# A second token pair's first feature tiles in seven products of halves instead of plain matmuls

## The chip, the cores and the metric

The kernel runs on one core of a Trainium2 chip, as one program. The metric is the device time of one execution in microseconds, lower is better; of the kernel before there are three runs. A profiled execution of its own gives the trace. Engine names in the rows: PE is TensorE's matmuls and PEld its weight loads, DVE is VectorE, ACT is ScalarE, POOL is GpSimd, SP is SyncE, whose queue issues every transfer here.

## The reference

```python
# attention: q, k, v are (4, 8, 576, 64) fp32
scores = (q @ k^T) / sqrt(64)
ret = (scores * Dmat) @ v               # Dmat[h, i, j] = gamma_h ** (i - j) where i >= j, else 0
x = ret, all heads side by side         # 2304 tokens x 512
# first layer, w_in 512 x 2048, w_out 2048 x 512
h = x @ w_in
x = (h * sigmoid(h)) @ w_out
# second layer, same sizes
h = x @ w_in2
g = max(h, 0) + alpha * min(h, 0)       # alpha: one number per feature
out = g @ w_out2
```

All of it is in fp32.

## The kernel before

**Matmuls.** An fp32 operand is kept as two tiles, a high and a low part (`split`: ScalarE casts the high part, VectorE subtracts it to get the low one). A product is three matmuls: high by high, low by high, high by low. The moving operand has 384 columns, half of a *token pair* of 768 tokens; there are three pairs (0, 1, 2).

**Feature tiles.** The 2048 features are 16 tiles of 128, taken two at a time (q = 0 to 7); two q make a group, and each layer has four groups. For one q and one token pair, 512 x 256 weights against 512 x 768 tokens, the work is done in one of two ways. *Plain* (`h_unit`): twelve matmuls for each of two feature tiles and two token halves, 48 in all. *Seven products of halves* (`products`): the weights and the tokens are cut in halves both ways, sums of the quarters are multiplied, seven products of six matmuls each, 42 in all. The weights' sums are made by `sums`, the tokens' seven operands B11, T1, B21, T2, B22, T3, T4 by `operands` (seven `split`s of 768 elements, by `put`, and four differences, by `less`, in place). They live in one set of tiles, `xop`, for the pair that is at work, and are stored to memory (`od`) and loaded again when the pair comes up next. The products share PSUM banks: the first and third use bank a, the second and fifth d, the first (by a copy on ScalarE), fourth, sixth and seventh b. Each must wait until what stood in its bank has been read: the seventh for the addition on VectorE that takes the sixth's result.

**The woven part.** Attention is done in 18 blocks of 128 tokens. Behind each block ScalarE copies the result to `ybuf`. While attention runs, the first group (four feature tiles) of pairs 0 and 1 is computed by plain units between the blocks, and then the output units y, twelve matmuls each that multiply activations by `w_out`. For this, `keep` (L548) splits each block of pairs 0 and 1 into its plain operands and stores it to memory (`xd`), from which `operands_again` makes the seven operands when the pair comes up in the second group. Pair 2 never has plain units: its operands are made by `operands` in the late part. The order on TensorE is written out in `EARLY_ORDER` and `LATE_ORDER` (L38 to L40) and followed by `follow`: `b` is a whole attention block (its first outputs, the next block's loads, scaling and scores, the next block's state, its second outputs), `h10` is one plain unit of pair 1's first half, `y01` one output unit of pair 0's second half, `s` the weights' sums for q = 0 and 1, `o` the operands of pair 2. `close_att` stands between the two orders: it gives back the attention's memory, in which the following tiles are then laid, among them the buffer `rawb` for weights.

**What sets the order elsewhere.** Every instruction is first recorded. TensorE's stand in the recorded order. For the other engines and SP's queue, `Program.order` plays the program through with rough costs and takes, among what can start, what is due first; each engine then works through its list strictly in that order. Alpha's load and the step that turns it into `nalpha_sb`, which only the second layer reads, are recorded behind the late order, and the planner puts them where they fit.

Of the kernel before, what the change touches and what calls it, by code (L numbers as in the profile page):

```python
# [9 lines left out]
F32 = mybir.dt.float32  # L10
# [8 lines left out]
P = 128  # L19
# [5 lines left out]
NC = DM // P  # L25
# [6 lines left out]
HALF = 384  # L32
NT6 = NT // HALF
NPR = NT6 // 2
BPP = 2 * HALF // P
PACKS = 3
EARLY = 8
EARLY_ORDER = ("w10 f g w4 i w3 l k j i w3 l w1 k j w2 i l j k h00 b h00 b h00 b h00 h01 b "  # L38
               "h01 b h01 b h01 b y00 y00 b y00 b y01 b y00 y01 y01 y01 b h10 h10 b h10 b h10 b b")
LATE_ORDER = "h11 h11 h11 h11 s o y10 y10 y10 y10"  # L40
PERIOD = 2 * S // P
WIDE = 3
SMALL = [C, 2 * C, C, NPAIR * C, P]
# [190 lines left out]
def retention_ffn_kernel(ctx: ExitStack, tc: tile.TileContext, qkv, w1, w2, alpha, small, out):  # L234
# [3 lines left out]
    dram = ctx.enter_context(tc.tile_pool(name="dram", bufs=1, space=bass.MemoryType.DRAM))  # L238
# [3 lines left out]
    nalpha_sb = const.tile([P, NF], F32, name="nalpha_sb")  # L242
    seven = const.tile([P, 1], F32, name="seven")
    ybuf = big.tile([P, NC * NT], F32, name="ybuf")
    xd = [dram.tile([P, NC * 2 * HALF], F32, name=f"xd{p}") for p in range(NPR - 1)]
    od = [[[dram.tile([P, 4 * HALF], F32, name=f"od{l}_{p}_{i}") for i in range(7)] for p in range(NPR)]
          for l in range(2)]

    def f32(t):
        return t.bitcast(F32)  # L250

    def feat(p):
        return ybuf[:, p * NC * 2 * HALF:(p + 1) * NC * 2 * HALF].rearrange("p (c t) -> p c t", c=NC)
# [23 lines left out]
    stock, lent = Store(), {}  # L277
# [18 lines left out]
    banks = [ps.tile([P, 512], F32, name=f"bank{i}") for i in range(4)]  # L296
    homes = {"a": banks[0:1], "b": banks[1:2], "d": banks[2:3], "o": banks[3:4]}
# [45 lines left out]
    def split(hi, lo, src):  # L343
        nc.scalar.copy(hi, src)
        nc.vector.tensor_tensor(out=lo, in0=src, in1=f32(hi), op=ALU.subtract)
# [45 lines left out]
    def sums(both, w):  # L391
        a21, a22, a11, a12 = (w[:, i * 256:(i + 1) * 256] for i in range(4))
        nc.vector.tensor_tensor(out=a22, in0=a21, in1=a22, op=ALU.add)
        nc.vector.tensor_tensor(out=a21, in0=a11, in1=a21, op=ALU.subtract)
        nc.vector.tensor_tensor(out=a11, in0=a22, in1=a11, op=ALU.subtract)
        nc.vector.tensor_tensor(out=a12, in0=a12, in1=a11, op=ALU.subtract)
        split(both[:, 0, 768:1792], both[:, 1, 768:1792], w)
# [107 lines left out]
    def att_out(n):  # L505
# [38 lines left out]
        inside(1)  # L544
        copy(1)
        keep(n, x)

    def keep(n, x):  # L548

        if n // BPP < NPR - 1:  # L550
            home = xd[n // BPP].rearrange("p (c t) -> p c t", c=NC)
            nc.sync.dma_start(out=home[:, :, n % BPP * P:(n % BPP + 1) * P], in_=x)
            first, second = PLAIN[n // BPP, n % BPP // 3]
            both = bass.AP(tensor=xop.tensor, offset=xop.offset + first * 4 * HALF + n % 3 * P,
                           ap=[xop.ap[0], (2 * HALF, 2), ((second - first) * 4 * HALF, 2), (HALF, 2), (1, P)])
            split(both[:, 0], both[:, 1], x.rearrange("p (i k) t -> p i k t", i=2))
# [37 lines left out]
    g_hi, g_lo, closing = {}, {}, []  # L594
# [42 lines left out]
    def operands(src):  # L637

        b11, b12, b21, b22 = (src[:, 2 * k:2 * k + 2, j * HALF:(j + 1) * HALF] for k in range(2) for j in range(2))
        put(B11, b11)  # L640
        less(b11, b12, b11)
        put(T1, b11)
        put(B21, b21)
        put(B22, b22)
        less(b12, b22, b12)
        less(b22, b22, b11)
        put(T2, b22)
        put(T3, b12)
        less(b21, b21, b22)
        put(T4, b21)  # L650

    def operands_again(p):

        halves = []
        for k, i in enumerate((T1, T3)):
            nc.sync.dma_start(out=f32(xops[i]), in_=xd[p][:, k * 4 * HALF:(k + 1) * 4 * HALF])
            halves += f32(xops[i]).rearrange("p (c j t) -> p j c t", c=2, j=2)[:, 0], \
                f32(xops[i]).rearrange("p (c j t) -> p j c t", c=2, j=2)[:, 1]
        b11, b12, b21, b22 = halves
        t, t3 = (u.rearrange("p (c t) -> p c t", c=2) for u in spare)  # L660
        put(B11, b11)
        less(t, b12, b11)
        less(t3, b22, b12)
        put(T1, t)
        put(B21, b21)
        put(B22, b22)
        less(t, b22, t)
        put(T2, t)
        less(t, b21, t)
        put(T3, t3)  # L670
        put(T4, t)
# [3 lines left out]
    def operands_for(layer, p, first):  # L675
        if loaded[-1] == (layer, p):
            return
        if first:
            operands(feat(p))
        else:  # L680
            if (layer, p) in kept:
                for i in (B11, T1, B21, T2, B22, T3, T4):
                    nc.sync.dma_start(out=f32(xops[i]), in_=od[layer][p][i])
            else:
                operands_again(p)
        if (layer, p) not in kept:
            for i in (B11, T1, B21, T2, B22, T3, T4):
                nc.sync.dma_start(out=od[layer][p][i], in_=f32(xops[i]))
            kept.add((layer, p))
        loaded.append((layer, p))  # L690
# [3 lines left out]
    def home(k):  # L694
        turns[k] += 1
        at = homes[k][turns[k] % len(homes[k])]
        return at if k == "o" else at[:, 0:HALF]
# [11 lines left out]
    def products(layer, q, key):  # L709


        weights(layer, q)
        both = w_pair[layer, q]
        f1, f2 = 2 * q, 2 * q + 1
        a, b, d = home("a"), home("b"), home("d")
        s5, s2 = [], []

        def first():
            product(a, both, A11, B11, start=True)
            nc.scalar.copy(b, a)  # L720

        def second():
            product(d, both, S1, T1, start=True)
            s5.append(rings["act"].next())
            nc.scalar.copy(s5[0], d)

        def third():
            product(a, both, A12, B21)
            activate(layer, f1, (*key, 0), a)

        def fourth():
            product(b, both, S2, T2)
            s2.append(rings["act"].next())
            nc.scalar.copy(s2[0], b)

        def fifth():
            product(d, both, S4, B22)
            nc.vector.tensor_tensor(out=d, in0=d, in1=s2[0], op=ALU.add)
            activate(layer, f1, (*key, 1), d)

        def sixth():
            product(b, both, S3, T3)
            nc.vector.tensor_tensor(out=s5[0], in0=b, in1=s5[0], op=ALU.add)
            activate(layer, f2, (*key, 1), s5[0])

        def seventh():
            product(b, both, A22, T4)
            activate(layer, f2, (*key, 0), b)

        return dict(zip("adABDCE", (first, second, third, fourth, fifth, sixth, seventh)))  # L750
# [98 lines left out]
    def with_done(pieces, key, fs):  # L849
        return pieces[:-1] + [lambda: (pieces[-1](), done(key, fs))]  # L850
# [11 lines left out]
    def begin_banks():  # L862
        both = w_pair[0, 0]
        for o in homes["b"]:
            nc.tensor.matmul(o[:, 0:HALF], both[:, 0, 0:P], xops[B11][:, 0:HALF], start=True, stop=True,
                             skip_group_check=True)
# [4 lines left out]
    plan = {}  # L871
    for p in range(2):
        for th in range(2):
            key = (0, p, th)
            plan[f"h{p}{th}"] = [lambda p=p, th=th, f=f: h_unit(p, th, f) for f in fs]
            plan[f"y{p}{th}"] = with_done([e for m in range(NC) for e in y_pieces(key, fs, p, th, m, 1)], key, fs)
    loaded.append(None)

    def follow(order):
        for e in order.split():  # L880
            if e == "h10" and not closing:
                closing.append(True)
                stock.free[:] = [g for g in stock.free if id(g) not in lent]
            if e == "b":
                for part in "ilkj":
                    att_part(part)
            elif e in "ilkj":
                att_part(e)
            elif e == "f":
                att_next(0)  # L890
            elif e == "g":
                att_sums(0)
            elif e[0] == "w":
                warm(int(e[1:]))
            elif e == "o":
                operands_for(0, 2, True)
            elif e == "s":
                for q in range(2):
                    sums(w_pair[0, q], whole[q])
            else:  # L900
                plan[e].pop(0)()

    follow(EARLY_ORDER)
    homes["o"] = banks[3:4]
    close_att()
    follow(LATE_ORDER)
    begin_banks()
    queue += plan["y11"]
# [3 lines left out]
    for n, (gi, layer, qs, p) in list(enumerate(steps))[2:]:  # L912
# [3 lines left out]
        for th in range(2):  # L916
            key = (gi, p, th)
            if layer == 0:
                e = [y_pieces(key, fs, p, th, m, 2) for m in range(NC)]
            else:  # L920
                e = [out_pieces(key, fs, p, th * 3 + b, n == len(steps) - 1 and th == 0 and b == 2) for b in range(3)]
# [84 lines left out]
```

## Time and profile before

| | us |
|---|---|
| median of 3 runs (lowest, highest) | 820.06 (819.90, 820.44) |
| profiled execution | 820.67 |
| its span on the core | 818.8 |
| TensorE busy (share of the span) | 806.6 (99%) |
| VectorE busy | 545.3 (67%) |
| ScalarE busy | 482.9 (59%) |
| moved by the transfers | 152.84 MB |

The page's granted clock of TensorE is at 9 tenths or more in every slice. A busy share of 99% means that TensorE's idle time is a few microseconds in all, each piece of which can be found in its list of waits. The other engines idle for a third of the time or more, but each works through its list in a fixed order, so that one instruction that waits holds up all behind it.

### The profile page before, as it was taken

What the parts mean: (1) busy time and instruction counts of PE and PEld (TensorE: products, weight loads), DVE (VectorE), ACT (ScalarE), POOL (GpSimd) and SP (SyncE); (2) the same over time, 40 slices, a digit from 0 to 9 for tenths busy, and PEclk for the clock granted to TensorE, in tenths of its full rate; (3) what the DMA queues carried; (4) which work ended last, traced back from release to release, by engine and by line L of the source; (5) the groups of instructions that cost most, each with busy time, mean ns of one, the idle gap of its engine ahead of it and who ended that gap; (6) DMA issues with size and microseconds to landing.
All of it is one profiled execution on the core that took longest, in us unless ns stands there. A gap on an engine that the chain in (4) does not pass through costs nothing.

```text
span 818.8 us, 14920 instructions
## 1 busy us (share of the span) xinstructions
PE 806.6 (99%) x6077; PEld 759.3 (93%) x6077; DVE 545.3 (67%) x928; ACT 482.9 (59%) x912; POOL 0.7 (0%) x5
## 2 busy tenths in 40 slices
PE   8899999999999999999999999999999999999998
PEld 5788999999999999999999899899898898898897
DVE  6887497578876534764379887784568952763653
ACT  4683388987876743675366588885256652342340
POOL 0000000000000000000000000000000000000000
PEclk9999999999999999999999999999999999999999
DMA  9996364358844861185635637176503751054802
GB/s 337 355 324 215 106 243 184 100 193 323 277 162 141 298 240 42 53 258 201 235 155 186 252 129 270 59 282 215 216 2 98 274 198 73 1 179 161 304 39 91
DMA packets 54933, 152.84 MB, mean 187 GB/s; under 512 B 5712, under 2 KB 12112, under 8 KB 54864
## 3 DMA queue, kind: packets, MB, share of 16 engines
q1 hardware_dynamic: 54864, 151.88, 52.5%
q8 instruction: 48, 0.79, 0.4%
q14 instruction: 21, 0.17, 0.1%
HBM read 110.96 MB, written 40.89 MB: 185 GB/s over the span
## 4 chain that ended last, share of the span: by engine, by line
PE 95%; DVE 3%; DMA 1%; issue 1%; ACT 0%; SPq 0%; DVEq 0%
PE bank L230 46%; PE late L230 45%; PE xo L230 2%; PE sd L230 2%; DMA pack<-in_qkv 1%; DVE pack L230 1%; DVE wt L230 1%; DVE wk L230 0%; DVE w L230 0%; DVE ybuf L230 0%; DVE att L230 0%; ACT low L230 0%; SPq L230 0%; ACT ybuf L230 0%; ACT xop L230 0%
## 5 line engine op out<-in xcount | busy, mean ns | idle before, releaser
L230 PE MATMUL bank<-xop,w 128*128 128x384 f32 x955 | 189.8, 335 | 1.6 <-DVE act L230 0.9
L230 PEld LDWEIGHTS bank<-xop,w 128*128 128x128 f32 x955 | 168.0, 188 | 5.4 <-DVE act L230 1.2
L230 DVE TENSOR_TENSOR ybuf<-late,ybuf 128x384 f32<-128x384 f32 (+2 forms) x85 | 51.4, 607 | 54.9 <-PE late L230 54.0
L230 PE MATMUL late<-xop,w 128*128 128x384 f32 x409 | 80.7, 334 | 0.0
L230 PEld LDWEIGHTS late<-xop,w 128*128 128x128 f32 x409 | 71.8, 188 | 0.0
L230 PE MATMUL bank<-xop,w0b 128*128 128x384 f32 x360 | 71.3, 335 | 0.0
L230 PE MATMUL late<-g,w 128*128 128x384 f32 x310 | 69.3, 334 | 0.0
L230 PEld LDWEIGHTS bank<-xop,w0b 128*128 128x128 f32 x360 | 63.5, 188 | 1.2
L230 PE MATMUL late<-w,g 128*128 128x512 f32 (+1 forms) x213 | 58.2, 386 | 0.0
L230 ACT COPY late<-bank 128x384 f32<-128x384 f32 x22 | 10.2, 465 | 78.3 <-PE bank L230 78.1
L230 PEld LDWEIGHTS late<-g,w 128*128 128x128 f32 x310 | 55.1, 188 | 0.0
L230 PE MATMUL late<-xop,w0b 128*128 128x384 f32 x270 | 53.6, 334 | 0.0
L230 PE MATMUL late<-w1b,g 128*128 128x512 f32 (+1 forms) x182 | 50.0, 384 | 0.0
L230 ACT ACTIVATE act<-bank 128x384 f32<-128x384 f32 x60 | 29.5, 491 | 30.7 <-PE bank L230 23.7
L230 PEld LDWEIGHTS late<-xop,w0b 128*128 128x128 f32 x270 | 47.4, 188 | 0.0
L230 ACT ACTIVATE low<-low,seven 128x512 int32<-128x512 f32 x64 | 46.0, 721 | 0.3
L230 PEld LDWEIGHTS late<-w,g 128*128 128x128 f32 x213 | 39.5, 188 | 7.2
L230 DVE TENSOR_TENSOR ybuf<-bank,ybuf 128x384 f32<-128x384 f32 (+1 forms) x42 | 25.8, 613 | 30.4 <-PE bank L230 30.1
L230 PE MATMUL bank<-g,w 128*128 128x384 f32 x206 | 44.3, 335 | 0.0
L230 DVE TENSOR_TENSOR g<-act,g 128x384 fp32r<-128x384 f32 x63 | 34.7, 553 | 14.1 <-ACT g L230 14.1
L230 ACT CAST g<-act 128x384 fp32r<-128x384 f32 x70 | 35.8, 515 | 9.7 <-DVE act L230 8.7
L230 PE MATMUL late<-g,w1b 128*128 128x384 f32 x167 | 41.2, 334 | 0.0
(163 smaller groups left out, 1530.3 us busy)
## 6 DMA issues: line engine op xcount, KB each, us to landing
xop<-od SPq DMA_DIRECT2D x70, 768.0 KB, 6.1
od<-xop SPq DMA_DIRECT2D x42, 768.0 KB, 4.3
pack<-in_qkv SPq DMA_DIRECT2D x64, 256.0 KB, 5.1
raw<-in_w SPq DMA_DIRECT2D x64, 256.0 KB, 3.5
rawb<-in_w SPq DMA_DIRECT2D x56, 256.0 KB, 3.8
out<-ybuf SPq DMA_DIRECT2D x17, 256.0 KB, 2.0
xd<-ybuf SPq DMA_DIRECT2D x12, 256.0 KB, 5.3
xop<-xd SPq DMA_DIRECT2D x4, 768.0 KB, 5.0
```

Of the source, the lines that this page charges most:

```text
L230: getattr(getattr(self.nc, name), method)(*args, **kwargs)
```

## The change

Pair 1's first group is now done by seven products for each of q = 0 and 1, fourteen in all (`p` in the orders), in place of eight plain units. `begin_banks` runs once ahead of them. Pair 1's operands are made by `operands` (`x`) as soon as its last block, block 11, is out, and stored at once; its blocks are no longer split one by one, nor stored to `xd`, and its second group loads the stored operands. The weights' sums `s` stand ahead of the first product. Eight of the products stand in the early order, woven with the last three blocks, six in the late one. At the beginning the first two plain units stand together, and blocks 3 and 4 behind them.

```diff
-EARLY_ORDER = ("w10 f g w4 i w3 l k j i w3 l w1 k j w2 i l j k h00 b h00 b h00 b h00 h01 b "
-               "h01 b h01 b h01 b y00 y00 b y00 b y01 b y00 y01 y01 y01 b h10 h10 b h10 b h10 b b")
-LATE_ORDER = "h11 h11 h11 h11 s o y10 y10 y10 y10"
+EARLY_ORDER = ("w10 f g w4 i w3 l k j i w3 l w1 k j w2 i l j k h00 h00 b b h00 b h00 h01 b h01 "
+               "b h01 b h01 b y00 y00 b y00 b x y00 b y01 y01 b y01 b y01 s p p p b p p p b p p b")
+LATE_ORDER = "p p p p p p o y10 y10 y10 y10"
...
-    xd = [dram.tile([P, NC * 2 * HALF], F32, name=f"xd{p}") for p in range(NPR - 1)]
+    xd = [dram.tile([P, NC * 2 * HALF], F32, name=f"xd{p}") for p in range(1)]
...
-        if n // BPP < NPR - 1:
+        if n < BPP:
...
+    plan["p"] = []
...
-            if e == "h10" and not closing:
-                closing.append(True)
-                stock.free[:] = [g for g in stock.free if id(g) not in lent]
...
+            elif e == "x":
+                operands_for(0, 1, True)
             elif e == "s":
+                closing.append(True)
+                stock.free[:] = [g for g in stock.free if id(g) not in lent]
                 for q in range(2):
                     sums(w_pair[0, q], whole[q])
+            elif e == "p":
+                if not plan["p"]:
+                    homes["o"] = banks[3:4]
+                    begin_banks()
+                    plan["p"] += [step for q in range(2) for step in products(0, q, (0, 1)).values()] + [None]
+                plan["p"].pop(0)()
```

On ScalarE, around the last output unit of pair 0 (the copy from `bank_154` before, from `bank_153` now; `xo` is the attention's result). Before:

```order
L230 COPY ybuf<-bank_154 128x384 [waits PE_49]
L230 COPY ybuf<-xo 128x2x2x64 [waits PE_49] x2
L230 ACTIVATE act_149<-bank_155 128x384 [waits PE_49]
L230 CAST g_141<-act_149 128x384 [waits Activation_49]
L230 ACTIVATE act_150<-bank_156 128x384 [waits PE_49]
```

Now:

```order
L230 COPY ybuf<-xo 128x2x2x64 [waits PE_49] x2
L230 CAST xop<-ybuf 128x768 [waits DVE_49] x2
L230 COPY ybuf<-bank_153 128x384 [waits PE_49]
L230 COPY bank_154<-bank_153 128x384 [waits PE_49]
L230 COPY act_148<-bank_155 128x384 [waits PE_49]
L230 ACTIVATE act_149<-bank_153 128x384 [waits PE_49]
```

Two operand casts, which wait for VectorE, now stand ahead of that copy, and the first product, which writes the same bank, waits for the copy.

On VectorE, around alpha's step (`nalpha_sb<-alpha_sb`), behind the last attention block; `w` are weights' low parts, `g` and `gb` activations' low parts, `xop` the operands' low parts. Before:

```order
L230 TENSOR_TENSOR w_0_123<-wt_119,w_0_123 128x1024 [waits Activation_49]
L230 TENSOR_TENSOR xop<-ybuf,xop 128x768 [waits DMAHW0_49,Activation_49]
L230 TENSOR_TENSOR xop<-ybuf,xop 128x768 [waits Activation_49]
L230 TENSOR_TENSOR g_137<-act_149,g_136 128x384 [waits Activation_49]
L230 TENSOR_TENSOR w_1_124<-wt_120,w_1_124 128x1024 [waits Activation_49]
L230 TENSOR_TENSOR g_139<-act_150,g_138 128x384 [waits Activation_49]
L230 TENSOR_SCALAR nalpha_sb<-alpha_sb 128x16 [waits DMAHW1_49]
L230 TENSOR_TENSOR xop<-ybuf,xop 128x768 [waits PE_49,Activation_49]
```

Now:

```order
L230 TENSOR_TENSOR g_134<-act_148,g_133 128x384 [waits Activation_49]
L230 TENSOR_SCALAR nalpha_sb<-alpha_sb 128x16 [waits DMAHW2_49]
L230 TENSOR_TENSOR xop<-ybuf,xop 128x768 [waits PE_49,Activation_49]
L230 TENSOR_TENSOR ybuf<-ybuf 128x2x384 [waits DVE_49]
L230 TENSOR_TENSOR xop<-ybuf,xop 128x768 [waits PE_49,Activation_49]
L230 TENSOR_TENSOR g_136<-actb_1824,g_135 128x384 [waits DMAHW4_49,DMAHW3_49,DMAHW6_49,DMAHW0_49,Activation_49]
L230 TENSOR_TENSOR bank_155<-bank_155,actb_1825 128x384 [waits PE_49]
L230 TENSOR_TENSOR actb_1823<-bank_154,actb_1823 128x384 [waits PE_49]
```

The weights' sums and one operand of pair 2 no longer stand ahead of alpha's step. Behind it now stands the addition from `bank_154` (the last row), which the last of the fourteen products waits for. On SP's queue alpha's load stands behind the two loads into `rawb` in both kernels.

## Rows read from the trace of the kernel before

**Rows 1.** The page, part 4: the chain that ended last, by engine.

```profile
PE 95%; DVE 3%; DMA 1%; issue 1%; ACT 0%; SPq 0%; DVEq 0%
```

**Rows 2.** TensorE's waits, longest sum first: us in total, times, longest us.

```profile
PE sd L230 <- DVE pack L230: 1.6, 2, 1.0
```

**Rows 3.** Timeline of TensorE, 103 to 121 us: start us, us, operation, shape, count.

```profile
112.50 4.32 PE L230 MATMUL late<-g,w 128*128 128x384 f32 x24
116.66 2.24 PE L230 MATMUL bank<-g,w 128*128 128x384 f32 x12
```

**Rows 4.** The same, 71 to 87 us ([idle before <-releaser] at the end).

```profile
72.46 0.69 PE L230 MATMUL xo<-pack,att 64*64 64x64 f32 x32
...
74.49 1.83 PE L230 MATMUL bank<-w,w 128*128 128x384 f32 x9
77.58 0.68 PE L230 MATMUL bank<-w,w 128*128 128x384 f32 x3 [1.25 <-issue]
78.10 6.43 PE L230 MATMUL bank<-g,w 128*128 128x384 f32 x36
```

**Rows 5.** The same, 99 to 105 us: the end of the last attention block.

```profile
102.08 0.85 PE L230 MATMUL xo<-pack,att 64*64 64x64 f32 x32 [0.51 <-ACT ybuf L230]
...
103.66 0.46 PE L230 MATMUL xo<-att,pack 64*64 64x64 f32 x16 [0.49 <-ACT ybuf L230]
104.05 1.16 PE L230 MATMUL bank<-xop,w 128*128 128x384 f32 x5
```

**Rows 6.** Stretches: length, busy PE, PEld, DVE, ACT, POOL; granted clock, DMA share, GB/s.

```profile
19.00:34.00 15.00, 12.84 (x347) 10.66 (x345) 13.65 (x25) 10.59 (x23) 0.00 (x0) 1.00 1.05 354
149.00:817.00 668.00, 666.61 (x3580) 631.42 (x3578) 430.42 (x730) 386.89 (x724) 0.00 (x0) 1.00 0.49 174
```

**Rows 7.** Timeline of VectorE, 74 to 81 us.

```profile
78.40 0.69 DVE L230 TENSOR_TENSOR pack<-pack,att 128x512 f32<-128x512 f32 x1 [1.34 <-DMA pack<-in_qkv]
```

**Rows 8.** VectorE's groups by form: busy us, mean ns of one, idle before.

```profile
L230 DVE TENSOR_TENSOR wt<-wt 128x256 f32<-128x256 f32 x64 | 26.9, 422 | 1.4
...
L230 DVE TENSOR_TENSOR xop<-ybuf,xop 128x768 fp32r<-128x768 f32 x28 | 26.4, 953 | 2.7 <-PE bank L230 1.6 <-ACT xop L230 0.8
...
L230 DVE TENSOR_TENSOR w<-wt,w 128x1024 fp32r<-128x1024 f32 x11 | 13.4, 1221 | 3.0 <-ACT w L230 2.7
...
L230 DVE TENSOR_TENSOR act<-bank,act 128x384 f32<-128x384 f32 x15 | 8.3, 554 | 2.0 <-PE bank L230 2.0
```

**Rows 9.** Timeline of VectorE, 114.5 to 121 us.

```profile
115.23 0.95 DVE L230 TENSOR_TENSOR ybuf<-ybuf 128x768 f32<-128x768 f32 x1
116.10 0.95 DVE L230 TENSOR_TENSOR xop<-ybuf,xop 128x768 fp32r<-128x768 f32 x1
```

**Rows 10.** ScalarE's groups by form.

```profile
L230 ACT CAST xop<-ybuf 128x768 fp32r<-128x768 f32 x28 | 23.3, 836 | 4.3 <-PE bank L230 3.6 <-DVE ybuf L230 0.7
...
L230 ACT COPY ybuf<-bank 128x384 f32<-128x384 f32 x13 | 6.2, 480 | 11.6 <-PE bank L230 11.3
```

**Rows 11.** Timeline of TensorE, 144 to 149 us.

```profile
145.09 1.21 PE L230 MATMUL bank<-xop,w 128*128 128x384 f32 x6
147.19 1.34 PE L230 MATMUL bank<-xop,w 128*128 128x384 f32 x6 [0.90 <-DVE act L230]
```

**Rows 12.** Timeline of SP's queue, 92 to 108 us.

```profile
104.23 1.85 SPq L230 DMA_DIRECT2D rawb<-in_w  x2
106.12 0.43 SPq L230 DMA_DIRECT2D alpha_sb<-in_alpha  x1
```

**Rows 13.** Transfers issued between 104 and 112 us: count, KB, median us to landing.

```profile
alpha_sb<-in_alpha SPq DMA_DIRECT2D x1, 8.0 KB, 2.4
```

**Rows 14.** Timeline of VectorE, 99 to 125 us.

```profile
110.70 0.17 DVE L230 TENSOR_SCALAR nalpha_sb<-alpha_sb 128x16 f32<-128x16 f32 x1
```

**Rows 15.** Timeline of TensorE, 0 to 16 us: the opening.

```profile
1.31 3.96 PE L230 MATMUL bank<-xop 128*128 128x512 f32 x10 [1.31 <-POOL xop L230]
...
14.66 0.96 PE L230 MATMUL bank<-xop 128*128 128x512 f32 x3
```

## The prediction

> **What bounds the kernel now.** I read the page's engines (the table above) and its chain of waits first: TensorE is busy for 99% of the span, and 95% of the chain that ended last is TensorE's own time [rows 1]. Then the list of TensorE's waits: its longest entry sums to 1.6 us [rows 2]. So the time is the sum of TensorE's instructions plus a handful of short waits, and any edit must be priced there: matmuls that go, waits that go, waits that come. In the timeline 24 matmuls of 384 columns pass between 112.50 and 116.66 us, 0.173 us each; a plain unit or an output unit y (12 matmuls) is 2.08 us, one product (6) 1.04 us [rows 3]. The waits that the change can reach are 1.25 us at 77.58, put down to issue alone [rows 4], 0.51 us where the last two attention blocks stand side by side and 0.49 us inside the last one [rows 5].
>
> **The change part by part.** *Matmuls.* Eight plain units of the second pair (96 matmuls) become fourteen products (84), and one more matmul opens a bank: 11 fewer, 11 x 0.173 = 1.9 us less [rows 3]. Up to the end of the last block the count is equal but for that one: four plain units before, eight products now. The gain lies in the late part: six products, 6.24 us, for four plain units, 8.32 us.
>
> *Start of the woven part.* The first two plain units now stand together and blocks 3 and 4 behind them. VectorE is busy for 13.65 of the 15 us there [rows 6], and what TensorE waits for next, the second weight tile and the scaled operands of block 5, comes from the same VectorE instructions in nearly the same order. I take 0; between -0.5 (the two units cover a wait) and +1.0 us (the two blocks side by side meet a VectorE queue that is not done).
>
> *What goes for the second pair.* Six stores of 256 KB, six casts on ScalarE and six subtractions on VectorE go from behind its blocks. At the second group's step of this pair, two loads and eighteen instructions that made the operands again become seven loads. From 149 to 817 us TensorE is busy for 666.6 of 668 us [rows 6], and ten such sets of seven loads already lie there; I take 0 for that exchange, and if the cover fails at most 1.0 us, the longest wait in rows 2.
>
> *The seven operands, made behind block 11.* Seven casts, seven subtractions and four differences of 768 elements, then seven stores of 768 KB on SP's queue. The stores stand between pack loads that are not needed for two blocks, so no load comes too late by them. The first product (p1) writes bank 0, which the last y unit has just filled. Its eviction stands on ScalarE behind two operand casts, which wait for VectorE. VectorE's queue from the operand of block 15, whose scaling began at 78.40, when it had landed, to the last of these differences holds 14 instructions: two scalings of a pack (0.69 each [rows 7]), one weight sum (0.42), one subtraction of 1024 (1.22), one mask of 512 (as a pack's scaling, 0.69), two state sums of the size of a weight sum, and six of 768 (0.95) [rows 8]. Started back to back they come 0.87 us apart for 0.95 of duration, so 0.08 less each [rows 9]: 2 x 0.61 + 0.42 + 1.14 + 0.61 + 2 x 0.34 + 6 x 0.87 = 9.3 us, to 87.7. The cast (0.84) and the eviction (0.48) follow [rows 10], with some 0.2 us of hand-over: p1 at 89.2. TensorE could be there at 74.49 + four units of 2.08 + two blocks of 2.03 (72.46 to 74.49) + some 0.5 us for changes of kind = 87.4 [rows 3, 4]. The six small stores are off the queues, so I put the landing 0.6 us earlier: p1 at 88.6, a wait of 1.2 us. The least is 0.6 (the eviction alone), the most 1.8 us. The wait of 1.25 us at 77.58 lies ahead of it; if it stays, it is taken out of this one, because p1's time is set by VectorE. Early part: +0.17 (the opening matmul) -1.25 -0.51 +1.2 = -0.4 us, from -1.0 to +0.5. The last block's inner 0.49 us stays.
>
> *The six late products.* The last of them (p14) writes the bank that the sixth (p13) leaves, after VectorE has added from it, and nothing stands between. The trace has such a pair: 0.90 us of wait at 147.19 [rows 11]. But here VectorE's queue has other work ahead of that sum, first of all the scaling of alpha, which waits for alpha's transfer. That transfer stands on SP behind two raw loads into memory that the attention gives back: they start at 104.23, right behind the last attention matmul (103.66 + 0.46), alpha's issue at 106.12 [rows 5, 12], and it lands 2.4 us later [rows 13]: 4.5 us behind the end of the last block, T = 104.05. Before, VectorE came to it at 110.70 with no wait [rows 14], because sums, two subtractions of 1024 and activations stood ahead. Now all of these are done: it arrives at about T + 0.5 and stands. Behind it and ahead of p14's sum: two operand subtractions and a difference of the third pair (3 x 0.87), one activation's subtraction and an addition into a bank (0.5 each), then the sum itself (0.55) [rows 8, 9]. With alpha's own 0.17 that is 4.3 us, so the sum is done at T + 8.8 and p14 starts at T + 8.9. Five products and a change of kind end at T + 5.3: a wait of 3.6 us. Bounds: 0.9 (as in the pair at 147.19, if alpha is not what VectorE waits for) and 4.0 us (landing counted from the end of the issue, 0.43 later). I take 3.6, since each of its terms has a row. The y units that follow need p14's result only in their last three matmuls, 0.1 us. Late part: -2.08 + 3.6 + 0.1 = +1.6 us.
>
> *Sum.* -0.4 + 1.6 = +1.2 us. The profiled execution took 820.67 us (span 818.8 and 1.9 around it), 0.61 above the median of 820.06; on the median the forecast is 821.3 us.
>
> **The rivals.** *Alpha is not in the way.* If the transfer lands before VectorE comes to it, p14 waits 0.9 us and the late part is -1.1: in all -1.5, 818.6 us; with the least wait at p1, -2.1, 818.0. For it: alpha cost nothing before [rows 14]. Against it: it landed at 108.5 then, and the work that filled the time until 110.70 has been moved ahead.
>
> [...]
> [...]
>
> *The chain before p1 is longer than my sum* (slower). VectorE's queue of 14 leaves no gap, and each instruction in it may wait for ScalarE, which carries evictions between casts; a store of 768 KB may push a pack's landing back. 1.5 us more, the size of the waits for a pack's landing in this stretch (1.34 [rows 7]): 822.8 us. Against it: VectorE has been relieved of six subtractions just before.
>
> **How the numbers follow.** Forecast 0.47, alpha not in the way 0.17, slower clock 0.14, longer chain 0.16, something else 0.06. About 0.2% (1.64 us) is what a measurement of this kernel can tell from no change: 818.4 to 821.7. The forecast lies inside but near the upper edge; with bounds of some 0.8 us on its terms I give a third of it (0.16) to slower. Half of the alpha case is faster (0.085), nearly all of the other two slower (0.28), and most of the rest faster (0.045). So faster 0.13, same 0.43, slower 0.44. The forecast's own range is 820.0 to 822.3; the range for 8 in 10 takes in the cases on both sides, 818.4 to 823.8.
>
> **What would show it.** In the trace of the changed kernel: 11 matmuls fewer at the same 0.173 us; the fifth of the last six products followed by a wait for VectorE of 3 to 4 us ahead of the final one, and on VectorE an idle stretch of some 4 us that ends with alpha's scaling, released by its transfer; a wait of about 1 us on ScalarE's eviction ahead of p1; no new wait behind 150 us; and the y units behind p14 at 2.08 us (if they take longer, the clock rival holds). I am wrong if the wait ahead of p14 is near 0.9 us, or if TensorE reaches the end of the last block more than 1 us away from 103.6.

## The result, and the profile after

| | before | after |
|---|---|---|
| median of 6 runs each (lowest, highest), us | 820.37 (819.90, 821.89) | 825.16 (824.57, 827.32) |
| ratio to before, 95% interval | | 1.0055 (1.0044 to 1.0066) |
| profiled execution, us | 820.67 | 825.89 |
| its span, us | 818.8 | 824.0 |
| mean granted clock in it | 1.000 | 0.996 |

The change makes the kernel slower by 4.8 us. The forecast was 821.3 us, with 818.4 to 823.8 for 8 in 10: slower, but by 1.2 us. The page of the changed kernel, parts 1, 2 and 4 (of part 2 the granted clock in 40 slices of 20.6 us, in tenths):

```profile
PE 808.1 (98%) x6066; PEld 759.6 (92%) x6066; DVE 544.3 (66%) x926; ACT 481.9 (58%) x912; POOL 0.7 (0%) x5
...
PEclk9899999999999999999999999999999999999999
...
PE 95%; DVE 2%; DMA 1%; issue 1%; ACT 0%; SPq 0%; DVEq 0%
```

TensorE's matmuls are 11 fewer (6066 for 6077), its busy time is 1.5 us more (806.6 before). Fewer matmuls of the same kinds took longer in all; the second slice of the clock, an 8 among nines, says where to look. TensorE's waits, longest sum first (before: [rows 2]):

```profile
PE bank L230 <- DVE actb L230: 4.1, 2, 3.2
PE xo L230 <- ACT ybuf L230: 2.4, 4, 0.8
...
PE xo L230 <- issue: 1.3, 2, 1.0
PE bank L230 <- issue: 0.9, 1, 0.9
```

The wait of 3.2 us is that of p14, the last of the fourteen products. The timeline of TensorE behind the last block (before: [rows 3, 5], where the fourth y unit ends at the start of this row):

```profile
120.82 0.33 PE L230 MATMUL bank<-xop,w 128*128 128x384 f32 x1
```

Now:

```profile
107.27 5.50 PE L230 MATMUL bank<-xop,w 128*128 128x384 f32 x30
115.98 1.34 PE L230 MATMUL bank<-xop,w 128*128 128x384 f32 x6 [3.21 <-DVE actb L230]
117.16 1.72 PE L230 MATMUL late<-g,w 128*128 128x384 f32 x9
...
119.31 1.75 PE L230 MATMUL bank<-g,w 128*128 128x384 f32 x9
...
125.58 0.33 PE L230 MATMUL bank<-xop,w 128*128 128x384 f32 x1
```

T, the end of the last block, is 107.27; p14 starts at T + 8.71 (forecast T + 8.9), and the fourth y unit ends at 125.58. VectorE there, and SP's queue (start, length, operation):

```profile
107.27 0.56 DVE L230 TENSOR_TENSOR g<-act,g 128x384 fp32r<-128x384 f32 x1 [0.36 <-ACT g L230]
111.62 0.18 DVE L230 TENSOR_SCALAR nalpha_sb<-alpha_sb 128x16 f32<-128x16 f32 x1 [3.80 <-DMA alpha_sb<-in_alpha]
...
114.91 0.56 DVE L230 TENSOR_TENSOR bank<-bank,actb 128x384 f32<-128x384 f32 x1
```

```profile
107.40 0.80 SPq L230 DMA_DIRECT2D rawb<-in_w  x2
108.25 1.35 SPq L230 DMA_DIRECT2D alpha_sb<-in_alpha  x1
```

VectorE stands for 3.80 us until alpha lands, then makes the operands queued behind, then the sum that p14 needs. But T itself is 3.2 us later than before (104.05). TensorE at the start of the woven part, and stretches of the same execution (columns as in [rows 6]; the granted clock is the third number from the end):

```profile
30.24 0.46 PE L230 MATMUL xo<-att,ybuf 64*64 64x64 f32 x16 [0.84 <-ACT ybuf L230]
31.25 0.46 PE L230 MATMUL xo<-pack,att 64*64 64x64 f32 x16 [0.55 <-ACT ybuf L230]
...
32.11 1.28 PE L230 MATMUL sd<-pack 64*64 64x64 f32 x42 [0.17 <-DVE pack L230]
33.88 0.81 PE L230 MATMUL sd<-pack 64*64 64x64 f32 x19 [0.48 <-issue]
...
35.15 4.21 PE L230 MATMUL bank<-xop,w 128*128 128x384 f32 x12
```

```profile
32.00:40.00 8.00, 7.41 (x132) 6.62 (x136) 5.62 (x11) 3.84 (x10) 0.00 (x0) 0.57 1.05 376
...
114.00:122.00 8.00, 6.02 (x34) 5.89 (x35) 7.63 (x12) 6.97 (x14) 0.00 (x0) 1.00 0.90 368
```

Behind three short waits in blocks 3 and 4 (0.84, 0.55 and 0.17 us) the granted clock is at 0.50 from 32.8 to 39.6 us: a plain unit takes 4.2 us there, not 2.1. The fourth wait (0.48 us), which the expectation of old_start counts among them, comes when the clock is already down. Behind p14's wait the clock stays at 1.00 in this execution. Read alone, this trace says that the start is to blame. The experiments say that it is one place of two.

### The profile page after: what moved, and what is told of

Same layout as the page of the kernel before. It is cut to its first block, busy times and chain, and to the rows that moved or that the text cites. A ratio compares the mean times of both kernels' runs of the same rounds, so it can differ in the third digit from the quotient of the medians.

```text
span 824.0 us, 14902 instructions
## 1 busy us (share of the span) xinstructions
PE 808.1 (98%) x6066; PEld 759.6 (92%) x6066; DVE 544.3 (66%) x926; ACT 481.9 (58%) x912; POOL 0.7 (0%) x5
## 4 chain that ended last, share of the span: by engine, by line
PE 95%; DVE 2%; DMA 1%; issue 1%; ACT 0%; SPq 0%; DVEq 0%
PE bank L230 46%; PE late L230 45%; PE xo L230 2%; PE sd L230 2%; DMA pack<-in_qkv 1%; DMA alpha_sb<-in_alpha 0%; DVE wt L230 0%; DVE wk L230 0%; DVE ybuf L230 0%; DVE pack L230 0%; SPq L230 0%; DVE xop L230 0%; ACT low L230 0%; ACT ybuf L230 0%; DVE bank L230 0%
## 5 line engine op out<-in xcount | busy, mean ns | idle before, releaser
L230 PE MATMUL bank<-xop,w 128*128 128x384 f32 x986 | 196.5, 338 | 5.0 <-DVE actb L230 4.1
L230 PEld LDWEIGHTS bank<-xop,w 128*128 128x128 f32 x986 | 174.8, 189 | 9.3 <-DVE actb L230 4.8
L230 DVE TENSOR_TENSOR ybuf<-late,ybuf 128x384 f32<-128x384 f32 (+1 forms) x84 | 51.2, 609 | 48.9 <-PE late L230 47.8
L230 PE MATMUL late<-xop,w 128*128 128x384 f32 x391 | 77.2, 334 | 0.0
L230 PEld LDWEIGHTS late<-xop,w 128*128 128x128 f32 x391 | 68.7, 188 | 0.0
L230 PE MATMUL late<-w,g 128*128 128x512 f32 x216 | 60.0, 389 | 0.0
L230 DVE TENSOR_TENSOR ybuf<-bank,ybuf 128x384 f32<-128x384 f32 (+2 forms) x43 | 26.1, 607 | 43.2 <-PE bank L230 43.1
L230 ACT CAST g<-act 128x384 fp32r<-128x384 f32 x77 | 39.5, 514 | 11.5 <-DVE act L230 10.5
L230 PE MATMUL late<-w1b,g 128*128 128x512 f32 (+1 forms) x162 | 45.4, 387 | 0.0
L230 DVE SCALAR_TENSOR_TENSOR act<-act,nalpha_sb,bank 128x384 f32<-128x384 f32 x24 | 14.7, 611 | 40.8 <-ACT act L230 40.4
```

The lines of the kernel that those rows point to most:

```text
L230: getattr(getattr(self.nc, name), method)(*args, **kwargs)
```

## The experiments

The runs were made on three chips, each with its own runs of the kernel before: the first four kernels on one (median of before 820.94 us), the next four on another (821.01), the last three on a third (821.40). Times are compared by the ratio to before on the same chip. Before's own mean clock is 0.998 in 2 of 23, none of 23 and 2 of 17 executions there, and 0.999 or 1.000 in the others.

**old_start.** The changed kernel with the old order at the start.

```diff
-EARLY_ORDER = ("w10 f g w4 i w3 l k j i w3 l w1 k j w2 i l j k h00 h00 b b h00 b h00 h01 b h01 "
-               "b h01 b h01 b y00 y00 b y00 b x y00 b y01 y01 b y01 b y01 s p p p b p p p b p p b")
+EARLY_ORDER = ("w10 f g w4 i w3 l k j i w3 l w1 k j w2 i l j k h00 b h00 b h00 b h00 h01 b "
+               "h01 b h01 b h01 b y00 y00 b y00 b x y00 b y01 y01 b y01 b y01 s p p p b p p p b p p b")
```

> The changed kernel with the order at the start of the woven part put back (a plain unit, a block, a plain unit, a block, ...). Theory A, the start is where the time goes: in the changed kernel four waits between blocks 3 and 4 (0.84, 0.55, 0.17 and 0.48 us) are followed by a granted clock of 0.50 from about 32.8 to 39.4 us, and the fourth plain unit starts at 41.42 for 38.96 before. With the old order the clock stays at 1.00 there, that unit starts near 39.0, the last block ends near 104.8 and the time falls by 2.5 us to 822.7. Theory B, the VectorE chain ahead of the first product sets the time: that chain does not move with TensorE, the first product still starts near 92.5, its wait grows from 0.39 to 2 or 3 us, and the time stays at 825.2.

Measured: 827.1 us, ratio 1.0071 (1.0050 to 1.0093): no gain, so theory A in this form falls. Theory B isn't borne out either: the first product waits 0.39 us, as in the changed kernel. The start keeps its clock (1.00), but waits on issue are 4.93 us in this profile, and the clock falls behind p14:

```profile
116.99 2.29 PE L230 MATMUL bank<-xop,w 128*128 128x384 f32 x6 [4.34 <-DVE actb L230]
119.08 3.08 PE L230 MATMUL late<-g,w 128*128 128x384 f32 x9
```

```profile
116.00:120.00 4.00, 3.01 (x9) 3.01 (x10) 3.14 (x6) 2.30 (x6) 0.00 (x0) 0.53 0.94 382
```

The product takes 2.1 us (to 119.08) for 1.04, the next unit 3.84 (to 122.92) for 2.08. All six executions have a mean clock of 0.996 to 0.998.

**new_start_only.** The kernel before with the new order of the start alone.

```diff
-EARLY_ORDER = ("w10 f g w4 i w3 l k j i w3 l w1 k j w2 i l j k h00 b h00 b h00 b h00 h01 b "
-               "h01 b h01 b h01 b y00 y00 b y00 b y01 b y00 y01 y01 y01 b h10 h10 b h10 b h10 b b")
+EARLY_ORDER = ("w10 f g w4 i w3 l k j i w3 l w1 k j w2 i l j k h00 h00 b b h00 b h00 h01 b h01 "
+               "b h01 b h01 b y00 y00 b y00 b y01 b y00 y01 y01 y01 b h10 h10 b h10 b h10 b b")
```

> The kernel before with only the start of the woven part in the new order (two plain units, then blocks 3 and 4 side by side); no products, no other edit. Theory A (the start costs the time, by waits and by the lower clock behind them): slower by about 2.5 us, 822.8, with a granted clock of 0.5 for some 5 to 7 us near 33 to 40. Theory B (the start costs nothing without the rest of the change): within 0.5 us of 820.4.

Measured: 821.34 us, ratio 1.0005 (0.9992 to 1.0019): theory B in the median, but not in the clock. 6 of 12 executions had a mean clock of 1.000 and 6 of 0.995 to 0.998; the profiled one had 0.79 from 32 to 40 us, behind waits of 0.71, 0.69, 0.30 and 0.74 us. The new start lets the clock fall in some executions; a cost in the median is not shown.

**alpha_early.** The changed kernel with alpha's load moved.

```diff
             elif e == "x":
+                nc.sync.dma_start(out=alpha_sb, in_=alpha)
                 operands_for(0, 1, True)
...
-    nc.sync.dma_start(out=alpha_sb, in_=alpha)
```

> The changed kernel with alpha's transfer issued early in the program instead of behind the two raw loads; the step on VectorE that scales alpha stays where it stands. Theory A (alpha's transfer holds up VectorE and so the last product, p14): the 3.80 us of idle VectorE ahead of the scaling go, p14 waits 0.9 us instead of 3.2 as in the pair at 147.19 before, and the time falls by 2.3 us to 822.9. Rival (VectorE's queue behind alpha is long enough by itself, or the y units behind p14 find a new wait): p14 still waits over 2 us or the time falls by less than 1 us.

Measured: 821.96 us, ratio 1.0009 (0.9994 to 1.0023): theory A, and more than its 2.3 us (1.0055 less 1.0009 is 3.8 us). VectorE's scaling has no idle time ahead of it, and TensorE waits 0.65 us:

```profile
106.35 0.17 DVE L230 TENSOR_SCALAR nalpha_sb<-alpha_sb 128x16 f32<-128x16 f32 x1
```

```profile
112.01 1.31 PE L230 MATMUL bank<-xop,w 128*128 128x384 f32 x6 [0.65 <-DVE actb L230]
...
121.58 0.33 PE L230 MATMUL bank<-xop,w 128*128 128x384 f32 x1
```

The profiled execution keeps the clock at both places (1.00 in every stretch from 16 to 132 us), at the start behind waits as long as the changed kernel's:

```profile
30.51 0.46 PE L230 MATMUL xo<-att,ybuf 64*64 64x64 f32 x16 [1.06 <-ACT ybuf L230]
31.47 0.46 PE L230 MATMUL xo<-pack,att 64*64 64x64 f32 x16 [0.49 <-ACT ybuf L230]
...
34.47 2.36 PE L230 MATMUL bank<-xop,w 128*128 128x384 f32 x12
```

The mean clock is still 0.996 to 0.998 in 8 of the 12 executions; where it fell in them was not traced.

**filler_between_blocks.** The changed kernel with matmuls on unused operands where TensorE waits at the start.

```diff
-EARLY_ORDER = ("w10 f g w4 i w3 l k j i w3 l w1 k j w2 i l j k h00 h00 b b h00 b h00 h01 b h01 "
+EARLY_ORDER = ("w10 f g w4 i w3 l k j i w3 l w1 k j w2 i l j k h00 h00 i l k w4 j w3 i l w2 k j h00 b h00 h01 b h01 "
```

> The changed kernel with the new start, but nine matmuls of 512 columns on operands that are not used (4, 3 and 2 of them) put into the places between blocks 3 and 4 where TensorE waits. They cost about 0.22 us each, 2.0 in all, of which some 1.6 lie inside the waits. Theory clock (most of the loss at the start is the clock that falls behind these waits): the granted clock stays at 1.00 from 32 to 40, the plain unit that took 4.21 us takes 2.4, and the time falls by 1 to 2 us, to 823.2 to 824.2. Theory waits (the loss is the waits themselves, the clock's fall only goes with them): the time does not fall, 825.2 or above.

Measured: 826.07 us, ratio 1.0054 (1.0034 to 1.0075). The clock stays at 1.00 from 32 to 40 us, as the clock theory says; the time doesn't fall. In this profile the clock falls to 0.50 behind p14 (a wait of 3.06 us), and p1, the first product, waits 1.63 us for 0.39, so that the early part without issue is as long as in the changed kernel (104.61 us for 104.66, in the table below):

```profile
32.00:40.00 8.00, 7.69 (x231) 6.67 (x222) 6.95 (x13) 6.24 (x14) 0.00 (x0) 1.00 1.04 357
...
114.00:122.00 8.00, 6.80 (x23) 6.80 (x24) 6.69 (x11) 4.58 (x10) 0.00 (x0) 0.57 0.80 324
```

**after_again.** The changed kernel itself, for another profile and on the same chip as the next three.

> The changed kernel as it is, once more, beside the others of this call. So far two kernels with the same wait ahead of p14 had the granted clock at 0.50 for some 7 us behind that wait, while the first profile of the changed kernel had it at 0.50 from 33 to 39 us and at 1.00 behind the wait. Theory clock (either stretch can pull the clock down, which one differs from one execution to the next): ratio 1.0055 again, a mean granted clock of 0.995 to 0.998 in every execution, and 3.3 us or more lost to a clock of 0.50 in this profile too, at 33, behind p14 or at both. Rival (the loss at 33 to 39 us belongs to this order of instructions and is there in every execution): the clock is at 0.50 from 33 to 39 us again and at 1.00 behind p14.

Measured: 827.3 us, ratio 1.0073 (1.0052 to 1.0095), mean clock 0.994 to 0.996 in all six: the clock theory. The clock falls at both places:

```profile
32.00:36.00 4.00, 3.77 (x84) 3.47 (x85) 2.94 (x6) 2.36 (x7) 0.00 (x0) 0.57 1.06 382
...
114.00:122.00 8.00, 7.01 (x24) 7.02 (x25) 6.69 (x10) 4.59 (x10) 0.00 (x0) 0.57 0.77 314
```

```profile
106.02 5.50 PE L230 MATMUL bank<-xop,w 128*128 128x384 f32 x30
114.99 2.29 PE L230 MATMUL bank<-xop,w 128*128 128x384 f32 x6 [3.47 <-DVE actb L230]
117.07 3.08 PE L230 MATMUL late<-g,w 128*128 128x384 f32 x9
...
127.24 0.33 PE L230 MATMUL bank<-xop,w 128*128 128x384 f32 x1
```

So the same program loses the clock at the start alone in one execution and at both places in another.

**old_start_fill_p14.** old_start, and twelve matmuls on unused operands in p14's wait.

```diff
-LATE_ORDER = "p p p p p p o y10 y10 y10 y10"
+LATE_ORDER = "p p p p p w12 p o y10 y10 y10 y10"
```

> The changed kernel with the old start and twelve matmuls of 512 columns on operands that are not used between p13 and p14, where TensorE waits (3.2 us in the changed kernel, 4.3 us in the one with the old start alone, which took 827.1 us). They do not shorten the wait for VectorE; they only give TensorE work in it. Theory clock: the granted clock stays at 1.00 behind p14 in this profile, where it was 0.50 for 7 us, and the time is about 3.4 us below 827.1, 823.7. Rival (the lost time behind p14 is not due to the idle wait): the clock falls all the same, or the time stays within 1 us of 827.

Measured: 825.81 us, ratio 1.0066 (1.0047 to 1.0086). The half on the clock holds, 1.000 in 4 of 6 executions and all through the profile. The half on the time isn't shown: against old_start's 1.0071 there is no difference outside the intervals. The late part is 1.5 us shorter in the profile (20.57 for 22.11), less than the clock's fall behind p14 cost after_again (2.65 us, worked out below), since the first y unit now waits for its operands twice:

```profile
111.01 2.92 PE L230 MATMUL bank<-xop 128*128 128x512 f32 x12
114.72 1.31 PE L230 MATMUL bank<-xop,w 128*128 128x384 f32 x6 [0.79 <-DVE actb L230]
...
118.33 0.62 PE L230 MATMUL late<-gb,w 128*128 128x384 f32 x2 [0.74 <-ACT gb L230]
119.72 0.44 PE L230 MATMUL late<-gb,w 128*128 128x384 f32 x1 [0.76 <-DVE gb L230]
```

**old_start_alpha_early.** Both edits.

> The changed kernel with both edits: the old start, and alpha's transfer issued early. Theory clock: neither stretch that pulled the clock down is left, so the mean granted clock is 1.000 in nearly all executions, p14 waits under 1 us, and the time is that of before less 1.9 us of matmuls plus the waits on issue that the new arrangement brings (1 to 3 us): 820 to 822, and below alpha_early's 822.0 by the share of its executions that lost clock. Rival (the old start is worse by itself, since old_start took 827.1 us against some 825.2 for the changed kernel): slower than alpha_early by 1 us or more.

Measured: 821.95 us, ratio 1.0015 (0.9998 to 1.0033): in the range of the clock theory, but level with alpha_early. The theory's clock is not borne out: it was under 0.999 in 4 of 12 executions, so with the old start some executions lose it too. The profiled one (819.21 us) kept it and has only 0.40 us of issue waits.

**filler_alpha_early.** alpha_early with the nine fillers of filler_between_blocks.

> The changed kernel with alpha's transfer issued early and, between blocks 3 and 4, the nine filler matmuls. Theory clock: the clock stays at 1.000 in nearly all executions (alpha_early alone lost some in 9 of 12), so the time is 0.5 to 1.5 us below alpha_early, 820.5 to 821.5, though the fillers themselves cost up to 0.5 us. Rival (the clock's falls in alpha_early come from elsewhere): the mean clock is 0.996 to 0.998 in most executions, and the time is 822 or above.

Measured: 821.04 us, ratio 0.9997 (0.9985 to 1.0009), the clock under 0.999 in none of 12 executions, for 8 of 12 in alpha_early: the clock theory, as far as the clock goes. The time's interval overlaps that of alpha_early.

**before_b and before_c.** The kernel before, twice more, one execution each.

> The kernel before, once more, for its waits on issue alone. In the ten profiles so far these waits stand only at certain places of TensorE's program: after 473, 600, 728, 855, 981, 1109, 1490, 1617, 1744, 1871 and 1999 matmuls, that is 127 or a multiple of it apart, and each ends 2.2 to 2.7 us (3.3 at most) after the start of a transfer of 16 KB on the instruction queue. Theory A (the waits are TensorE's program arriving late, and how many come differs from one execution to the next): the same places again, but not the same waits as in the first profile of this kernel (0.16 at 981 and 1.25 us at 1616, 1.4 in all): 0.4 to 4 us in all. Theory B (this kernel's arrangement has few of them, the changed one many): 1.0 to 1.8 us in all again, at the same two places.

> The same kernel a third time, with the same expectation as the second: theory A 0.4 to 4 us of issue waits at places 127 matmuls apart, not the same as in the other two; theory B 1.0 to 1.8 us at 981 and 1616.

Measured: 821.28 and 821.56 us, issue waits of 2.40 and 2.86 us, not the same as in the first profile: theory A's forecast. Two rows of the one and two of the other:

```profile
54.54 0.34 PE L230 MATMUL xo<-att,pack 64*64 64x64 f32 x6 [1.26 <-issue]
73.58 1.22 PE L230 MATMUL bank<-g,w 128*128 128x384 f32 x6 [0.90 <-issue]
```

```profile
49.96 0.35 PE L230 MATMUL xo<-att,ybuf 64*64 64x64 f32 x9 [1.23 <-issue]
59.14 0.33 PE L230 MATMUL xo<-att,pack 64*64 64x64 f32 x3 [0.40 <-issue]
```

Counted from the program's start they stand behind 981 and 1489 matmuls, and behind 854 and 1108 (the other four at 600, 600, 1489 and 1616). At the place of the 1.25 us of [rows 4], behind 1616 matmuls, the one waits not at all and the other 0.16 us.

**old_start_alpha_early_fill.** The changed kernel with the old start, alpha early and six fillers.

```diff
-EARLY_ORDER = ("w10 f g w4 i w3 l k j i w3 l w1 k j w2 i l j k h00 h00 b b h00 b h00 h01 b h01 "
-               "b h01 b h01 b y00 y00 b y00 b x y00 b y01 y01 b y01 b y01 s p p p b p p p b p p b")
+EARLY_ORDER = ("w10 f g w4 i w3 l k j i w3 l w1 k j w2 i l j k h00 i w2 l k j h00 i w4 l k j h00 b h00 h01 b "
+               "h01 b h01 b h01 b y00 y00 b y00 b x y00 b y01 y01 b y01 b y01 s p p p b p p p b p p b")
```

> The changed kernel with the old start, alpha's transfer early, and six filler matmuls: two ahead of block 3's scores and four ahead of block 4's, where TensorE waits 0.52 and 0.64 to 1.0 us for VectorE. old_start_alpha_early without the fillers had a mean clock of 0.996 to 0.998 in 5 of its 12 executions. Theory clock: the clock stays near 1.000 in nearly all executions and the median falls to that of the undisturbed executions there, 820 to 821.3 us, level with the kernel before or a little under it. Rival (the clock's falls come from another place, or the fillers delay the blocks): 822 or above.

Measured: 820.69 us, ratio 0.9983 (0.9971 to 0.9996): it beats the kernel before by 0.17%, and so the changed one, with its ratios of 1.0055 and 1.0073, by 0.7 to 0.9%. 11 of 12 executions have a clock of 0.999 or 1.000, for 8 of 12 without the fillers (of those, four lost clock, not the five of the expectation). The fillers stand where VectorE is waited for, 0.66 and 1.14 us of work (from their start to the next matmul's) in the place of idle time:

```profile
26.09 0.73 PE L230 MATMUL bank<-xop 128*128 128x512 f32 x2
...
31.01 1.21 PE L230 MATMUL bank<-xop 128*128 128x512 f32 x4
```

## Why the prediction was wrong

One table from the profiled executions puts the steps apart, in us. T is the end of the last block; issue, the waits on issue up to T; "late", from T to the end of the fourth y unit; the last column, where the clock fell.

| execution | T | issue | T less issue | late | clock below 1.00 |
|---|---|---|---|---|---|
| before | 104.05 | 1.41 | 102.64 | 16.77 | - |
| before_b | 104.75 | 2.40 | 102.35 | 16.78 | - |
| before_c | 105.04 | 2.86 | 102.18 | 16.77 | - |
| after | 107.27 | 2.61 | 104.66 | 18.31 | start |
| after_again | 106.02 | 2.70 | 103.32 | 21.22 | start, behind p14 |
| old_start | 107.15 | 4.93 | 102.22 | 22.11 | behind p14 |
| new_start_only | 106.98 | 3.68 | 103.30 | 16.77 | start |
| alpha_early | 105.88 | 3.35 | 102.53 | 15.70 | - |
| filler_between_blocks | 106.66 | 2.05 | 104.61 | 20.78 | behind p14 |
| old_start_fill_p14 | 105.67 | 3.80 | 101.87 | 20.57 | - |
| old_start_alpha_early | 102.51 | 0.40 | 102.11 | 15.72 | - |
| filler_alpha_early | 106.09 | 2.43 | 103.66 | 15.75 | - |
| old_start_alpha_early_fill | 105.17 | 2.51 | 102.66 | 15.73 | - |

- **The six late products: right.** Without the clock the late part grew by 18.31 - 16.77 = 1.54 us, for a forecast of 1.6; p14's wait was 3.21 for 3.6. With alpha out of the way it shrank by 1.07, for the 1.1 of that rival, so the cause (alpha's load behind the raw loads, and the operands behind it on VectorE) is shown.
- **The clock: the step that failed.** My sum takes the full pace throughout, 0.173 us for a matmul, and I gave a slower clock 0.14, my estimate; no run at hand showed it fall behind a wait, or what that would cost. It is lower in all twelve executions of the changed kernel (a mean of 0.994 to 0.998). Behind p14 it costs 2.65 us in after_again (21.22 - 18.31, less the 0.26 by which that wait was longer), and nothing in the first profile, where it held at 1.00 behind p14. At the start the clock costs 0.8 to 2.1 us (103.32 and 104.66 for alpha_early's 102.53, which has the same order and kept the clock); it was low from 32.3 to 35.7 us in the one profile and from 32.8 to 39.6 in the other. There I took 0, up to 1.0, from VectorE's queue alone. TensorE's waits there are indeed not longer in sum (0.84 + 0.55 + 0.17 now, 0.52 + 1.04 + 0.17 before, without issue), but the clock falls to 0.50 behind them. Before:

```profile
27.00 1.11 PE L230 MATMUL sd<-pack 64*64 64x64 f32 x40 [0.52 <-DVE att L230]
...
32.94 0.69 PE L230 MATMUL sd<-pack 64*64 64x64 f32 x32 [1.04 <-DVE pack L230]
...
34.41 2.21 PE L230 MATMUL bank<-xop,w 128*128 128x384 f32 x11 [0.17 <-DVE w L230]
```

My ground for the low chance, the full pace behind a wait of 1.25 us (36 matmuls in 6.43 us [rows 4]), was one execution.

- **The 1.25 us at 77.58: the second step that failed.** I took it off the sum and let p1's wait be the shorter for it if it stayed; p1 waits 0.39 us and cannot take that in. And waits on issue differ from one execution to the next: the three profiles of before have 1.41, 2.40 and 2.86 us of them, the two of the changed kernel 2.61 and 2.70. By their means the early part becomes some 0.4 longer, not 1.25 shorter.
- **p1: right place, wrong waiter.** The wait is 0.39 us for 1.2, and 0.39 in all six other profiles of changed kernels without the nine fillers. VectorE's chain of 14 doesn't bind there: ScalarE is done with the two casts and itself waits for the last y unit before it evicts it:

```profile
91.93 0.48 ACT L230 COPY ybuf<-bank 128x384 f32<-128x384 f32 x1 [0.44 <-PE bank L230]
```

I had the eviction alone as the least, at 0.6. With the nine fillers VectorE does bind: in filler_between_blocks the two casts wait 1.91 and 0.63 us for it, the eviction follows them with no idle time, and p1 waits 1.63 us (1.07 in filler_alpha_early).

- **The early part without clock and issue** moved by -0.1 us between the first profile of before and alpha_early. The forecast's -0.4 holds the gain of 1.25; without that gain, and with the p1 wait as measured, it would be +0.05.
- **Behind the y units** some 0.4 us came on (from the fourth y unit to the span's end 698.4 for 698.0), within the 1.0 that was left for the exchanged loads; its cause was not looked for.

The sum for the first profile: issue +1.20, clock at the start +2.13, the rest of the early part -0.11, late part +1.54, behind it +0.44: 5.2 us, the difference of the spans. The forecast had -1.25, 0, +0.86, +1.6 and 0 for them: issue and the clock are what it lacks. T, at 107.27, is 3.7 us from the 103.6 that it named, more than the 1 us by which it would call itself wrong. For after_again against before_c: -0.16, +1.14 for the start with its clock, +4.45, +0.47: 5.9.

The median of 825.16 us is not taken apart in this way. The two executions around it (824.98 and 825.35 us) have a mean clock of 0.998, and by that the clock costs them at most some 2 us (an estimate: the share missing to 1.000, with its rounding, of a span of 823 us). They were not traced, so their waits on issue are not known.

What stays open is what decides in which execution the clock falls at a given place: behind p14 it stayed at 1.00 once after 3.21 us of idle time and fell after 3.06, 3.47 and 4.34; at the start it fell behind 0.84, 0.55 and 0.17 us, short one by one and with small matmuls between, and stayed in alpha_early's profile behind 1.06 and 0.49.

## What to carry to other kernels

Where TensorE is the bound, price a new wait twice: its own length, and the risk that the matmuls behind it run at a granted clock of 0.50 (2.65 us behind one wait here), and count several short waits close together as one place of that kind. Take no gain from a wait on issue that one trace shows. Look at the granted clock of every execution, not of one trace: a trace shows one of the places where the clock can fall, and mending that place alone may move nothing. A small load that a busy engine will wait for goes early in the queue. Fillers in waits that can't be removed kept the clock in 11 and 12 of 12 executions here; they take time of their own (103.66 us for 102.53 in the early part without issue, with the nine), and p1's wait was longer beside them.

## What the runs showed of the hardware that was not expected

I read the waits put down to "issue" as TensorE's program arriving late; no run changed how it is loaded, so this is an inference from what follows. In the thirteen profiles they stand behind 473, 600, 728, 855, 981, 1109, 1490, 1617, 1744, 1871, 1999 or 2125 matmuls (to within one), steps of 127 or its multiples. In the first profiles of the two kernels each of the six ends 2.3 to 2.5 us after the start of a transfer of 16 KB on the instruction queue, which takes 0.9 to 1.0 us; so does the longest of all, old_start's 2.01 us (2.3 to 2.4). For the changed kernel's wait of 0.96 us that ends at 51.90, the queue's row for the stretch 49.3 to 49.5 us (packets, MB, share), and TensorE's row:

```profile
q8 instruction: 1, 0.02, 32.1%
```

```profile
51.90 0.34 PE L230 MATMUL xo<-att,ybuf 64*64 64x64 f32 x8 [0.96 <-issue]
```

Of the 49 waits 37 stand in an attention block, whose matmuls are small and many (64x64 in this row). They sum to 0.4 to 4.9 us, where the forecast of this change was 1.2, and shift from one execution to the next. The counts agree with transfers that each bring a stretch of the program: 6077 matmuls for 48 of them before and 6066 for 47 now, 127 and 129 to one (an estimate: the division of the pages' counts). Few of them are waited for, four in the changed kernel's first profile; over the thirteen profiles a wait costs 0.16 to 2.01 us. Why the waits stand at one place in one execution and at another in the next was not tried.
